# Small constant stores into the result, placed among the loads of a decode-attention kernel

## The chip, the core and the metric

The kernel runs on one core of a Trainium2 chip. A core has five engines that run their own instruction streams: PE (TensorE, matmul), DVE (VectorE), ACT (ScalarE), POOL (GpSimd) and SP (SyncE, which here only starts transfers). Transfers between HBM and the on-chip memory SBUF are done by 16 DMA engines. The metric is the device time of one execution in microseconds (us); lower is better.

## The reference

One decode step of a block in which attention and an MLP work on the same normalised input, and their results are summed:

```python
x = A_x                                   # 1 x 1 x 1024
xn = _layernorm(x, axis=-1)
return x + _A_ref(xn, A_k_cache, A_v_cache, A_wq, A_wo) + _B_ref(xn, B_w1, B_w2, B_w3, B_w4)

def _A_ref(x, k_cache, v_cache, wq, wo):  # 32 query heads, 4 key/value heads, 65536 cached positions, 128 wide
    q = x @ wq
    p = _softmax(q @ k * 128 ** -0.5)
    return (p @ v) @ wo
def _B_ref(x, w1, w2, w3, w4):
    x1 = x + shifted(_gelu(_layernorm(x) @ w1)) @ w2    # with one position only zeros are left of the shifted part
    return x1 + _gelu(_layernorm(x1) @ w3) @ w4
```

Everything is bfloat16 in HBM. The caches are 2 x 67 MB, the weights 36 MB; the result is 1024 values, 2 KB.

## The kernel before, in words

The kernel is written engine by engine. A helper `_op` puts an instruction on an engine's list and works out from buffer objects (`_B`) which semaphores it has to wait for; `_dma` does the same for a transfer, on SP's or ACT's list. A transfer's semaphore is named by a channel (`chan("k0")`), and each transfer adds 16 to it when it has landed. Lists are emitted in order, so an engine that waits holds up all that stands behind it on its list.

**Loads.** One SBUF tensor, `KV`, holds four slots: two of 4 MiB for K and two of 8 MiB for V. All loads but that of x are issued by SP, in this order: wq, the first K, the first V, the second K (before the loop), and then, in a loop over 32 tiles n, what `issue_k` (L341) and `issue_v` (L349) give out:

```python
if n % 2:
    issue_k((n + 3) // 2)
if n % 4 == 1:
    issue_v((n + 3) // 4)
```

A K load covers two tiles and a V load four. Each waits until its slot has been read: `issue_k` waits for `QK` (L511) of the tile that has just used the slot, and `issue_v` for `PV` (L557). The transfers that SP has started stand in one queue, q1, and ACT's in another, q10. Near the end of the loop the weights w1, w2 and w3 of the MLP take over freed slots (n == 29), then wo and the first part of w4 (n == 31); after the loop the three last parts of w4 (L327).

**A tile.** `Ttr` transposes the tile's part of K in place on DVE (four instructions, L501). `QK` multiplies it with the queries into `S_ps`. `stats1`, `MB` and `stats2` form the running maximum; `EXP` makes the exponentials on ACT (L539) and the correction factor. `PTr` permutes and transposes them; `PV` multiplies with V into `OT_ps`; `FLASH` copies on ACT (L565) and accumulates on POOL. The engines other than SP run the tiles as hardware loops: `q_act.mark()` and its like mark where a loop's bodies begin and end, and what an engine is given behind the last mark runs once, after its loop.

**The end.** The w1 product (L639) with its GELU (L480 to L486; the Tanh on ACT is L484), the w2 product (L647), the second layer norm, the heads' combination, w3 (L472) with another GELU, wo (L681), w4 (L460). DVE copies the sums into `orow` (L717), and SP stores `orow` as four rows of 256 values (L718):

```python
ev_out = _dma(q_sp, chan("out"), lambda e: e.dma_start(out=out[0, 0, :].rearrange("(j n) -> j n", j=4), in_=orow[0:97:32, :]), reads=[b_p[0]])
q_sp.wait(ev_out)
```

`ones_f` is a 128 x 128 float32 tile of ones that GpSimd fills at the start; `b_const` is the buffer object of all such constants.

Of the kernel before, what the change touches and what calls it, by code (L numbers as in the profile page):

```python
# [6 lines left out]
BF = mybir.dt.bfloat16  # L7
# [113 lines left out]
def _deps(q, reads, writes):  # L121
    need = {}
    for b in reads:
        for s, v in b.w.items():
            need[s] = max(v, need.get(s, 0))
    for b in writes:

        for s, v in (list(b.r.items()) if b.r and b.whole else list(b.w.items()) + list(b.r.items())):
            if not (q.in_order and s is q.sem):
                need[s] = max(v, need.get(s, 0))  # L130
    for s, v in need.items():
        q.wait((s, v))


def _done(ev, reads, writes, partial=False):
    for b in reads:
        b.add_read(ev)
    for b in writes:
        if partial:
            b.add_write(ev)  # L140
        else:
            b.set_write(ev)


def _op(q, fn, reads=(), writes=(), partial=False, tick=True):
    _deps(q, reads, writes)
    ev = q.op(fn, tick)
    _done(ev, reads, writes, partial)
    return ev
# [17 lines left out]
def _dma(q, chan, fn, reads=(), writes=(), partial=False):  # L167
    _deps(q, reads, writes)
    chan.n += 1
    ev = q.dma(fn, chan.sem, 16 * chan.n)  # L170
    _done(ev, reads, writes, partial)
    return ev


def bass_parallel_sum__gqa_block_cached__mixer_s_mlp__decode_kernel(
# [32 lines left out]
    with ExitStack() as es:  # L208
        E = es.enter_context

        def sb(name, shape, dt):
            return E(nc.sbuf_tensor(name, shape, dt))
# [4 lines left out]
        def sem(name):  # L217
            return E(nc.semaphore(name))

        ident_bf = sb("ident_bf", [P, P], BF)  # L220
        ones_f = sb("ones_f", [P, P], F32)
# [68 lines left out]
        q_act = _Q("act", sem("c_act"))  # L290
        q_pool = _Q("pool", sem("c_pool"))
        q_sp = _Q("sp", None)
# [5 lines left out]
        def chan(name):  # L298
            if name not in chans:
                chans[name] = _DmaChan(sem("d_" + name))  # L300
            return chans[name]

        b_const = _B("const")
# [39 lines left out]
        def issue_v(j):  # L343
            if j >= NV:
                return
            h, nb = divmod(j, NV // HKV)
            src = A_v_cache[0, h, nb * 4 * SUB:(nb + 1) * 4 * SUB, :].rearrange("(p c) d -> p (c d)", p=P)
            sl = j % 2
            _dma(q_sp, chan("v%d" % sl), lambda e: e.dma_start(out=KV[:, VOFF[sl]:VOFF[sl] + 32768], in_=src), writes=[b_V[sl]])  # L349
# [59 lines left out]
        for c0, n_, lhs, rhs in ((0, P, selGT[:, :], selGT[:, :]), (P, P, selGT[:, :], selPT[:, :]),  # L409
                                 (256, 4, selTT[:, :], ident_bf[0:4, 0:4]), (260, 16, selDT[:, :], ident_bf[0:16, 0:16])):  # L410
            _op(q_pe, lambda e, c0=c0, n_=n_, lhs=lhs, rhs=rhs: e.matmul(CM_ps[:, c0:c0 + n_], lhs, rhs, start=True, stop=True),
                reads=[b_const, b_pT], writes=[b_CM], partial=(c0 > 0))
# [23 lines left out]
        for h in range(HKV):  # L436
            for we in range(4):
# [3 lines left out]
                    reads=[b_M1, b_const], writes=[b_Y], partial=(h + we > 0))  # L441
# [50 lines left out]
        def Ttr(n, idx):  # L492
            if n >= NT:
                for ix in idx:
                    q_dve.op(lambda e, ix=ix: e.memset(spare[:, ix:ix + 1], 0.0))
                return
            s, half = (n // 2) % 2, n % 2
            for ix in idx:
                c = KOFF[s] // 2 + 4096 * half + 1024 * ix
                _deps(q_dve, [b_K[s][half]], [])  # L500
                ev = q_dve.op(lambda e, c=c: e.transpose(out=KV32[:, c:c + 1024], in_=KV32[:, c:c + 1024]))  # L501
                b_T[s][half].add_write(ev)

        def QK(n):
            s, half = (n // 2) % 2, n % 2
            fns = []
            for we in range(4):
                w_hi, e_ = divmod(we, 2)
                for cm in range(4):
                    mv = bass.AP(KV[:].tensor, KOFF[s] + half * 8192 + cm * 128 + w_hi * 64 + e_, [[kstep, P], [512, 16], [2, 32]])  # L510
                    fns.append(lambda e, we=we, cm=cm, mv=mv: e.matmul(  # L511
                        S_ps[32 * cm:32 * cm + 32, :], Ycur[:, we, :, :].rearrange("p a g -> p (a g)"), mv,
                        start=(we == 0), stop=(we == 3), tile_position=(0, 32 * cm)))
            _grp(q_pe, fns, reads=[b_T[s][half], b_Yc], writes=[b_S])

        def stats1(n):
            m = n % 2
            _op(q_dve, lambda e: e.reduce_max(mrow[:, m:m + 1], S_ps[:, :], axis=AX.X), reads=[b_S], writes=[b_mrow[m]])  # L518
            _op(q_dve, lambda e: e.tensor_tensor(out=Rm[:, m, :], in0=sel16[:, :], in1=mrow[:, m:m + 1].broadcast_to([P, 16]), op=ALU.mult),  # L519
                reads=[b_mrow[m], b_const], writes=[b_R[m]])  # L520

        def MB(n):
            m = n % 2
            _op(q_pe, lambda e: e.matmul(MB_ps[:, 0:16], Lmat[:, :], Rm[:, m, :], start=True, stop=True),  # L524
                reads=[b_R[m], b_const], writes=[b_MB])

        def stats2(n):
            _op(q_dve, lambda e: e.tensor_reduce(out=Bst[:, n % 4:n % 4 + 1], in_=MB_ps[:, 0:16], axis=AX.X, op=ALU.min),  # L528
                reads=[b_MB], writes=[b_Bcol[n % 4]])

        def EXP(n):
            m = n % 2
            ko = 1 - m
            cL = 513 * m
            if n % 4 == 0:
                q_dve.wait((s_b, n // 4 + 1))
            _op(q_dve, lambda e: e.tensor_tensor(out=brun[:, m:m + 1], in0=brun[:, ko:ko + 1], in1=Bst[:, n % 4:n % 4 + 1], op=ALU.min),  # L537
                reads=[b_brun[ko], b_Bcol[n % 4]], writes=[b_brun[m]])
            _op(q_act, lambda e: e.activation(p_sb[:, m, :], S_ps[:, :], ACTF.Exp, bias=brun[:, m:m + 1], scale=SCALE, accum_out=tmpO[:, cL:cL + 1]),  # L539
                reads=[b_S, b_brun[m]], writes=[b_p[m], b_tmpL[m]])  # L540
            _op(q_dve, lambda e: e.tensor_tensor(out=dd[:, m:m + 1], in0=brun[:, m:m + 1], in1=brun[:, ko:ko + 1], op=ALU.subtract),  # L541
                reads=[b_brun[ko], b_brun[m]], writes=[b_dd[m]])
            _op(q_act, lambda e: e.activation(ff[:, m:m + 1], dd[:, m:m + 1], ACTF.Exp), reads=[b_dd[m]], writes=[b_ff[m]])  # L543
# [48 lines left out]
        for n in range(NT):  # L592
            if n % NSUB == 0:
                q_pe.mark(const_sems)
                q_pool.mark()
            if n % 4 == 0:
                q_act.mark()
            if n % 4 == 2:
                q_dve.mark(const_sems)
            if n == 0 or n % 4 == 2:  # L600
                Ttr(n, range(4))
            ahead = n + 1 if n % 4 != 1 else None
            if n % 4 != 1:
                QK(n)
            if ahead:
                Ttr(ahead, [0])
            stats1(n)
            MB(n)
            stats2(n)
            EXP(n)  # L610
            if ahead:
                Ttr(ahead, [1])
            PTr(n)
            if ahead:
                Ttr(ahead, [2, 3])
            if n % NSUB == NSUB - 1:
                head_switch(n // NSUB + 1)
            if n % 4 == 0:
                QK(n + 1)
            PV(n)  # L620
            FLASH(n)
            if n % NSUB == NSUB - 1:
                head_end(n // NSUB)
            if n % 2:
                issue_k((n + 3) // 2)
            if n % 4 == 1:
                issue_v((n + 3) // 4)
            if n == NT - 3:
                load_at(KOFF[0], b_K[0][:1] + b_T[0], "w1", B_w1, 0, 8)
                load_at(KOFF[0] + 8192, b_K[0][1:], "w2", B_w2, 0, 8)  # L630
                b_epi.r.update(b_V[0].r)
                load_at(VOFF[0], [b_V[0]], "w3", B_w3, 0, 8)
            if n == NT - 1:
                load_at(VOFF[1], [b_V[1]], "wo", A_wo, 0, 32)
                load_at(KOFF[1], b_K[1] + b_T[1], "w40", B_w4, 0, 16)
        for q in (q_pe, q_pool, q_act):
            q.mark(const_sems)

        _grp(q_pe, [lambda e, j=j, q=q: e.matmul(M0_ps[32 * q:32 * q + 32, :], xn2_bf[:, j:j + 1].broadcast_to([P, 32]),  # L639
                                                 KV[:, j * D + 512 * q:j * D + 512 * (q + 1)],  # L640
# [38 lines left out]
        def half_rows(items, reads):  # L679
# [12 lines left out]
            reads=[b_cb], writes=[b_keep])  # L692
# [3 lines left out]
            reads=[b_OT, b_const], writes=[b_pT])  # L696
# [6 lines left out]
            reads=[b_M0, b_M1], writes=b_ge)  # L703
# [11 lines left out]
        out_rows(*w4_rows(2))  # L715
        out_rows(*w4_rows(3), last=True)
        _op(q_dve, lambda e: e.tensor_copy(orow, OUT_ps[:, 0:256]), reads=[b_OUT], writes=[b_p[0]])  # L717
        ev_out = _dma(q_sp, chan("out"), lambda e: e.dma_start(out=out[0, 0, :].rearrange("(j n) -> j n", j=4), in_=orow[0:97:32, :]), reads=[b_p[0]])  # L718
        q_sp.wait(ev_out)

# [33 lines left out]
```

## Time and profile before

| what | value |
|---|---|
| time, median of 2 runs | 400.58 us (400.48 to 400.67) |
| time of the profiled execution | 400.37 us |
| its span | 399.0 us |
| busy: PE, DVE, ACT, POOL | 44%, 59%, 12%, 23% of the span |
| read from HBM | 169.87 MB, 426 GB/s over the span |
| share of q1 (SP's transfers) in the DMA engines' time | 98.7% |
| from issue to landing, median: K, V | 23.7 us, 36.1 us |

The profile shows one execution. Its span runs from the first to the last recorded instruction; the time of the same execution is 1.4 us longer. Engines are named as above, and PEld is PE's weight load; "SPq" is SP issuing a transfer, which ends long before the transfer lands. A row of digits gives the busy share in 40 equal slices of the span, in tenths. The chain of waits follows the work that ended last back to its beginning; a "DMA" piece in it runs from the issue of a transfer to its landing, so it holds the time in the queue too. A packet is one contiguous piece that one DMA engine moves; besides the data there are 4-byte packets that increment the transfer's semaphore.

### The profile page before, as it was taken

How to read it: one execution, taken by the hardware profiler on the slowest of the kernel's cores; microseconds unless marked ns; L12 is line 12 of the kernel's file. 1: busy time of each engine (PE TensorE's matmuls, PEld its weight loads, DVE VectorE, ACT ScalarE, POOL GpSimd, SP SyncE). 2: the span in 40 equal slices, each digit the busy share in tenths (PEclk: the TensorE clock that was granted, in tenths of full speed). 3: DMA queues.
4: the chain of work that ended last, by engine and by line, in shares of the span. 5: the costliest groups of instructions: out<-in, count | busy, mean ns of one | idle time of the engine just before them, and what ended most of it. 6: DMA issues, size and time to landing. Idle time of an engine off the chain costs nothing.

```text
span 399.0 us, 4487 instructions
## 1 busy us (share of the span) xinstructions
PE 175.9 (44%) x1456; PEld 53.1 (13%) x1456; DVE 235.4 (59%) x403; ACT 49.1 (12%) x132; POOL 91.6 (23%) x173
## 2 busy tenths in 40 slices
PE   0044244455254525442544464245426442572775
PEld 0022111111011101110111111011101110121322
DVE  0024756784688388728864886487657756635411
ACT  1000020111021101110201020111021120110000
POOL 6000012232135212230253021304331222251000
PEclk9997555555556656665655556656555655567699
DMA  8989999999999999999999999999999999999995
GB/s 355 486 368 473 416 418 424 434 429 443 470 422 394 447 440 420 427 447 466 427 407 434 440 420 440 434 466 427 411 430 440 434 434 406 456 459 421 419 409 247
DMA packets 4912, 169.98 MB, mean 426 GB/s; under 512 B 676, under 2 KB 680, under 8 KB 808
## 3 DMA queue, kind: packets, MB, share of 16 engines
q1 hardware_dynamic: 4760, 169.87, 98.7%
q8 instruction: 5, 0.08, 0.1%
q10 hardware_dynamic: 144, 0.00, 0.0%
q14 instruction: 3, 0.02, 0.0%
HBM read 169.87 MB, written 0.00 MB: 426 GB/s over the span
## 4 chain that ended last, share of the span: by engine, by line
DMA 57%; DVE 18%; PE 13%; issue 10%; ACT 1%; another core or an unknown queue 0%; POOL 0%; DVEq 0%; SPq 0%; ACTq 0%; POOLq 0%
DMA KV<-in_A_k_cache_dram 42%; DVE KV L501 13%; DMA KV<-in_B_w_dram 9%; PE S_ps L511 8%; DMA x_bf<-in_A_x_dram 6%; DVE mrow L518 2%; PE PT_ps L547 2%; PE OT_ps L557 1%; PE MM_ps L639 1%; ACT p_sb L539 1%; DVE pT_f L549 1%; PE MB_ps L524 1%; PE MM_ps L647 0%; DVE Rm L519 0%
## 5 line engine op out<-in xcount | busy, mean ns | idle before, releaser
L501 DVE STREAM_TRANSPOSE KV<-KV 128x1024 f32<-128x1024 f32 x128 | 149.5, 1211 | 23.9 <-DMA KV<-in_A_k_cache_dram 23.9
L511 PE MATMUL S_ps<-KV,Ycur 128*32 128x512 bf16 x512 | 59.5, 613 | 84.4 <-DVE KV L501 84.0
L570 POOL TENSOR_TENSOR O_acc<-O_acc,tmpO 128x513 f32<-128x513 f32 x32 | 40.8, 1275 | 121.9 <-ACT tmpO L565 121.9
L557 PE MATMUL OT_ps<-KV,pT_f 128*32 128x512 bf16 x512 | 58.9, 610 | 19.5 <-DVE pT_f L549 18.7
L518 DVE TENSOR_REDUCE mrow<-S_ps 128x1 f32<-128x512 f32 x32 | 22.1, 691 | 38.4 <-PE S_ps L511 38.4
L539 ACT ACTIVATE p_sb<-S_ps,brun 128x512 bf16<-128x512 f32 x32 | 22.0, 687 | 137.7 <-DVE brun L537 137.7
L547 PE MATMUL PT_ps<-p_sb,permR 128*128 128x512 bf16 x32 | 17.3, 541 | 44.5 <-ACT p_sb L539 44.5
L565 ACT ACTIVATE tmpO<-OT_ps 128x512 f32<-128x512 f32 x32 | 19.2, 599 | 136.8 <-PE OT_ps L557 78.3
L511 PEld LDWEIGHTS S_ps<-KV,Ycur 128*32 128x32 bf16 x512 | 14.4, 126 | 125.3 <-DVE KV L501 96.3
L549 DVE STREAM_TRANSPOSE pT_f<-PT_ps 128x512 f32<-128x512 f32 x32 | 22.7, 709 | 12.1 <-PE PT_ps L547 11.4
L567 POOL TENSOR_TENSOR spare<-ff 128x1 f32<-128x1 f32 x32 | 6.2, 193 | 102.0 <-ACT ff L543 100.3
L568 POOL TENSOR_SCALAR O_acc<-O_acc,ff 128x514 f32<-128x514 f32 x32 | 22.4, 701 | 0.0
L557 PEld LDWEIGHTS OT_ps<-KV,pT_f 128*32 128x32 bf16 x512 | 15.7, 130 | 50.6 <-DVE pT_f L549 28.9
L524 PE MATMUL MB_ps<-Rm,Lmat 128*128 128x16 bf16 x32 | 6.1, 191 | 25.3 <-DVE Rm L519 25.3
L528 DVE TENSOR_REDUCE Bst<-MB_ps 128x1 f32<-128x16 f32 x32 | 5.6, 174 | 14.2 <-PE MB_ps L524 14.2
L389 PE MATMUL MM_ps<-ln_s,ones_f 128*128 128x1 f32 x6 | 1.8, 362 | 27.0 <-DVE ln_s L388 27.0
L385 DVE CAST xT<-x_bf 128x8 f32<-128x8 bf16 x1 | 0.2, 170 | 21.3 <-DMA x_bf<-in_A_x_dram 21.3
L401 POOL TENSOR_TENSOR ln_s<-ln_s,neghalf 128x1 f32<-128x1 f32 x3 | 1.7, 558 | 40.5 <-DVE ln_s L399 40.5
L524 PEld LDWEIGHTS MB_ps<-Rm,Lmat 128*128 128x128 bf16 x32 | 3.3, 102 | 52.5 <-DVE Rm L519 52.5
L547 PEld LDWEIGHTS PT_ps<-p_sb,permR 128*128 128x128 bf16 x32 | 3.2, 101 | 47.3 <-ACT p_sb L539 47.3
L541 DVE TENSOR_TENSOR dd<-brun 128x1 f32<-128x1 f32 x32 | 5.7, 178 | 3.6
L537 DVE TENSOR_TENSOR brun<-brun,Bst 128x1 f32<-128x1 f32 x32 | 5.5, 172 | 3.7
(117 smaller groups left out, 123.4 us busy)
## 6 DMA issues: line engine op xcount, KB each, us to landing
KV<-in_A_k_cache_dram SPq DMA_DIRECT2D x16, 4096.0 KB, 23.7
KV<-in_B_w_dram SPq DMA_DIRECT2D x1, 7168.0 KB, 33.7
KV<-in_B_w_dram SPq DMA_DIRECT2D x2, 2048.0 KB, 15.1
KV<-in_B_w_dram SPq DMA_DIRECT2D x1, 4096.0 KB, 34.8
KV<-in_B_w_dram SPq DMA_DIRECT2D x1, 1536.0 KB, 34.0
KV<-in_B_w_dram SPq DMA_DIRECT2D x1, 1024.0 KB, 36.0
KV<-in_B_w_dram SPq DMA_DIRECT2D x1, 512.0 KB, 36.8
KV<-in_A_v_cache_dram SPq DMA_DIRECT2D x8, 36.1
```

The costliest lines, as they stand in the source:

```text
L501: ev = q_dve.op(lambda e, c=c: e.transpose(out=KV32[:, c:c + 1024], in_=KV32[:, c:c + 1024]))
L511: fns.append(lambda e, we=we, cm=cm, mv=mv: e.matmul(S_ps[32 * cm:32 * cm + 32, :], Ycur[:, we, :, :].rearrange("p a g -> p (a g)"), mv, s ...
L518: _op(q_dve, lambda e: e.reduce_max(mrow[:, m:m + 1], S_ps[:, :], axis=AX.X), reads=[b_S], writes=[b_mrow[m]])
L524: _op(q_pe, lambda e: e.matmul(MB_ps[:, 0:16], Lmat[:, :], Rm[:, m, :], start=True, stop=True), reads=[b_R[m], b_const], writes=[b_MB])
L539: _op(q_act, lambda e: e.activation(p_sb[:, m, :], S_ps[:, :], ACTF.Exp, bias=brun[:, m:m + 1], scale=SCALE, accum_out=tmpO[:, cL:cL + 1]) ...
L547: _op(q_pe, lambda e: e.matmul(PT_ps[:, :], permR[:, :], p_sb[:, m, :], start=True, stop=True), reads=[b_p[m], b_const], writes=[b_PT])
L549: _op(q_dve, lambda e: e.transpose(out=pT_f[:, :], in_=PT_ps[:, :]), reads=[b_PT], writes=[b_pT])
L557: fns.append(lambda e, q=q, q4=q4: e.matmul(OT_ps[32 * q4:32 * q4 + 32, :], pT_bf[:, q, :, 1], KV[:, v0 + 512 * q:v0 + 512 * (q + 1)], sta ...
L565: _op(q_act, lambda e: e.activation(tmpO[:, 1:513], OT_ps[:, :], ACTF.Copy), reads=[b_OT], writes=[b_tmpO])
L567: q_pool.op(lambda e: e.tensor_tensor(out=spare[:, 4:5], in0=ff[:, m:m + 1], in1=ff[:, m:m + 1], op=ALU.add), False)
L568: b_Oacc.set_write(q_pool.op(lambda e: e.tensor_scalar(out=O_acc[:, :], in0=O_acc[:, :], scalar1=ff[:, m:m + 1], scalar2=0.0, op0=ALU.mult ...
L570: ev = q_pool.op(lambda e: e.tensor_tensor(out=O_acc[:, m:m + 513], in0=O_acc[:, m:m + 513], in1=tmpO[:, m:m + 513], op=ALU.add), tick=(s_ ...
```

## The change

In tile 17, behind the loads of that tile, SP issues six stores of parts of `ones_f` into the result; ACT issues a seventh behind its loop. The shapes differ: four rows from partitions 0, 32, 64, 96; four rows from neighbouring partitions; one row; 16 rows; 128 rows of 4 bytes; and again four rows from partitions 0, 32, 64, 96. In all they write 2,048 bytes. Before the final store, which writes the whole result, SP waits for both channels, so the constants are overwritten.

```diff
             if n % 4 == 1:
                 issue_v((n + 3) // 4)
+            if n == 17:
+                o1 = out[0, 0, :]
+                for a, src in ((0, ones_f[0:97:32, 0:16]), (128, ones_f[0:4, 0:16]), (256, ones_f[0:1, 0:64]), (384, ones_f[0:16, 0:4]), (512, ones_f[:, 0:1]),
+                               (768, ones_f[0:97:32, 16:32])):
+                    rows = src.bitcast(BF)
+                    dst = o1[a:a + rows.shape[0] * rows.shape[1]].rearrange("(j n) -> j n", j=rows.shape[0])
+                    ev_o1 = _dma(q_sp, chan("o1"), lambda e, rows=rows, dst=dst: e.dma_start(out=dst, in_=rows), reads=[b_const], writes=[_B()])
...
         for q in (q_pe, q_pool, q_act):
             q.mark(const_sems)
+        ev_o2 = _dma(q_act, chan("o2"), lambda e: e.dma_start(out=out[0, 0, 896:1024].rearrange("(j n) -> j n", j=4), in_=ones_f[0:97:32, 0:16].bitcast(BF)),
+                     reads=[b_const], writes=[_B()])
...
         _op(q_dve, lambda e: e.tensor_copy(orow, OUT_ps[:, 0:256]), reads=[b_OUT], writes=[b_p[0]])
+        q_sp.wait(ev_o1)
+        q_sp.wait(ev_o2)
         ev_out = _dma(q_sp, chan("out"), ...)
```

## The prediction

> **What bounds the kernel now.** I read the page first (its rows of slices and its table of queues), then the chain of waits, then SP's timeline around the place of the change, then the end. The page:
>
> ```profile
> span 399.0 us, 4487 instructions
> DMA  8989999999999999999999999999999999999995
> DMA packets 4912, 169.98 MB, mean 426 GB/s; under 512 B 676, under 2 KB 680, under 8 KB 808
> q1 hardware_dynamic: 4760, 169.87, 98.7%
> q10 hardware_dynamic: 144, 0.00, 0.0%
> ```
>
> The 16 DMA engines are busy in nine tenths or more of nearly every slice, and 98.7% of their time goes to one queue, q1, which SP fills. The chain of waits shows what hangs on it (columns: start, length, what):
>
> ```profile
> 230.32 1.93 PE S_ps L511 x16
> 232.33 23.78 DMA KV<-in_A_k_cache_dram
> 256.13 0.06 DVE KV L501
> ...
> 269.04 1.93 PE S_ps L511 x16
> 271.05 23.75 DMA KV<-in_A_k_cache_dram
> ...
> 359.63 36.78 DMA KV<-in_B_w_dram
> ```
>
> The chain names PE and DVE between the loads, but those steps only set when a load is put into the queue. When it lands is set by what stands ahead of it. A load of K is 4 MiB and a load of V 8 MiB; one round of four tiles is two of K and one of V, 16.78 MB, and K landings in the chain lie 38.7 us apart (256.11 and 294.80): 433.8 GB/s. By that rate 4 MiB takes 9.7 us, so of the 23.8 us of the load issued at 232.33 some 14 us are waiting in the queue. The weights go on in the same way: between 333.4 (last K) and 396.4 (last part of w4) 27.26 MB move, 432.8 GB/s. The queue is thus never empty from the second load to 396.4, and a microsecond that the slowest DMA engine loses anywhere in it comes out at the end. That engine is the resource; compute has slack.
>
> **The change, part by part.** It removes nothing. It adds six stores on SP behind the loads of n == 17, one store on ACT behind its loop, and two waits on SP ahead of the final store.
>
> *The issue on SP.* SP's timeline around the place, and the end:
>
> ```profile
> 209.83 0.33 SPq L341 DMA_DIRECT2D KV<-in_A_k_cache_dram  x1
> 210.21 0.42 SPq L349 DMA_DIRECT2D KV<-in_A_v_cache_dram  x1
> ...
> 232.33 0.33 SPq L341 DMA_DIRECT2D KV<-in_A_k_cache_dram  x1
> ...
> 397.36 0.62 SPq L718 DMA_DIRECT2D out_dram<-p_sb  x1
> ```
>
> The loads at 209.83 and 210.21 are issue_k(10) and issue_v(5) of n == 17 (the eleventh K, the sixth V); the next, issue_k(11), leaves at 232.33 when QK(19) has freed its slot. SP is idle from 210.63 to 232.33, 21.7 us. A store's issue is the last row: 0.62 us; six are 3.7 us, done by 214.4. What is queued behind them on SP is issue_k(11) alone, which is not due for another 17.9 us; were that cover gone, its 14 us in the queue would still hide 3.7 us. Cost 0. The constants were written by GpSimd in the first 10 us, so the wait for them passes at once.
>
> *The packets in q1.* A load of 128 rows is 128 packets and 16 increments of its semaphore: the x load alone makes q10's 144. The 33 loads of q1 (16 K, 8 V, wq, wo, 7 parts of B's weights) make 33 x 144 = 4752; the final store's four rows make the other 8, four rows and four increments. So the stores of 4, 4, 1, 16, 128 and 4 rows add 8 + 8 + 2 + 32 + 144 + 8 = 202. The 128-row and 16-row stores reach all 16 engines: 8 + 1 and 1 + 1 = 11 packets on each. An engine that gets a row of every store carries 19. They stand between the sixth V, which lands at 210.21 + 36.1 = 246.3, and the K that lands at 256.11. The trace's packet records price small packets in this same busy queue: a 4-byte increment takes 9 ns and the next load's first packet begins 6 ns after it; x's 16-byte rows take 9 ns, among packets of 65,536 bytes; the final store's 512-byte rows take 28 to 32 ns. So 11 packets at 9 ns are 0.1 us on every engine, the slowest too, and 19 are 0.17 us. I take 0.1.
>
> *The write receipts.* This is what no row shows: a store into HBM with loads right behind it on the same engine. Its increment can only follow the landed row; whether the engine holds the next load meanwhile is open. The low bound is nothing: 33 loads have such an increment, in 6 ns each, and no later packet is lengthened (1213 ns for nearly all of 32 KB). The high bound is the final store, whose landing SP awaited:
>
> ```profile
> SPq L718 <- DVE p_sb L717: 37.3, 1, 37.3
> SPq L57 <- DMA out_dram<-p_sb: 1.0, 1, 1.0
> ```
>
> 1.0 us from the end of the issue; the packet records put 0.6 of it ahead of the first packet and 0.4 from the first packet to SP. Six in a row, each held for 1.0 us, are 6.0 us; held for 0.4, 2.4 us. There is a cover for some of it: the 16 engines do not finish together. The sixth V's increments run from 244.25 to 246.08 in the packet records, so an engine can be up to 1.8 us ahead, and a loss on it alone is free up to that lead. Between 0 and 6.0 I take 0.4, one receipt for the batch, since the loads' increments are the nearest row (same queue, same engines, same traffic) and they hold nothing.
>
> *A bound below nothing.* The lead of 1.8 us has a cause that the change might shift: the packet records show instruction fetches (q8, q14; 8 and 16 KB, 0.3 to 1.0 us each) at 44, 55, 85, 116, 366, 378 and 394 us, each on one engine beside its loads. A program a few instructions longer may fetch on other engines. If none fell on the slowest, the end would come up to 1.8 us sooner; one more would cost up to 1.0 us. I take 0.
>
> *The store on ACT, and the waits.* ACT around its place:
>
> ```profile
> 353.99 0.60 ACT L565 ACTIVATE tmpO<-OT_ps 128x512 f32<-128x512 f32 x1 [3.41 <-PE OT_ps L557]
> 359.80 0.63 ACT L484 ACTIVATE KV<-KV 64x512 f32<-64x512 f32 x1 [5.21 <-DVE KV L483]
> ```
>
> ACT issues at about 354.6 and then idles 5.2 us for DVE; the x load's issue on ACT took 0.40 us. Behind it stands the Tanh at 359.80, not late. On its engines q10 takes turns with q1: x's 9 packets per engine landed in 22.0 us, 2.4 us a turn, so one row and one increment are in by some 361 us. SP's two waits come after its issue at 359.2 and before the wait for L717 (37.3 us): both events are old by 397.36. Cost 0; if the ACT store were not in, the final store would wait for it, but it has 36 us.
>
> Sum: 0 + 0.1 + 0.4 + 0 + 0 = 0.5 us. The profiled execution took 400.37 us, of which 399.0 are span and 1.4 lie around it; it stands 0.2 below the median of 400.58. So the changed kernel's profile should show 400.9, and its median 401.1.
>
> **The rivals.** What this kernel's measurement can tell from no change is about 2%, 8.0 us.
>
> *Receipts one after another.* Every store's increment stops its engine until the row has landed, and one engine carries all six. For it: the ring is read in order. Against it: the 6 ns behind loads. With 1.0 us each it is 6.0 us, 406.6; with the 1.6 us from issue to landing, 9.7 us, 410.3. From 1.34 us a store it is over 2%.
> The Trainium skill ("DMA: Bandwidth & Descriptors", the section on the anatomy of one DMA) puts most of a transfer's fixed 2 us into the receipt of the write, heaviest for HBM. No row here shows 2 us; by that figure six would be, as an estimate, 12 us.
>
> *Short rows, on the other side: slower.* The place is the 128-row store: 8 rows of 4 bytes on every engine, all into the same 512 bytes. If a row so short is read, merged and written back before the next, every engine, the slowest too, pays 8 round trips, and one more for the 16-row store. At the final store's 1.0 us that is 9.0 us, 409.6; with the other four stores on one engine 13.0, 413.6. It decides from 0.9 us a row. For it: no write this small is in the trace. Against it: packets of 4 and 16 bytes at 9 ns, though reads or increments.
> The Trainium skill (same page, Specifications) says that below 512 bytes the DMA engine does a read-modify-write. Only the final store, at just 512 bytes a row, is shown here.
>
> *Nothing, or a little gain.* All loss falls into the lead, or the fetches shift: 398.8 to 400.6.
>
> *Late loads.* The stores hold SP or the queue so long that issue_k(11) is late past its 14 us of backlog. The six would need 21.7 + 14 us instead of 3.7; then the cost would start from there. That the change does nothing is no separate case: its packets must appear.
>
> **How the numbers follow.** Forecast (0.2 to 3 us more): 0.58. Nothing or a little gain: 0.14. Receipts in a row: 0.14, of it 0.06 over 2%. Short rows: 0.10. Anything else: 0.04, half on each side of 2%. So slower by over 2% is 0.06 + 0.10 + 0.02 = 0.18; faster 0.02, since the queue already moves 433.8 GB/s and 8 us would need 2% more; within 2% 0.80. The range starts at 399.5, inside the gain case, and ends at 408.6, past receipts at 1.0 us; it leaves out some 0.16 above and 0.04 below. The forecast's own range is 400.6 to 403.6.
>
> **What would show it right or wrong.** Right: SP shows six issues between 210.6 and 215 and still idles until its next K at about 232.3; that K lands at 256.1 to 257; q1 counts 4962 packets and q10 152; K landings further on are again 38.7 us apart; the last weight lands near 397. Receipts or short rows: the K behind the stores lands at 262 or later, all after it by as much, and the slice at 246 to 256 us moves fewer GB/s. Late loads: SP's issues run past 232. The forecast is wrong if the K issued at 232.3 takes over 27 us to land, or if the time is lost or won after 350 us, at ACT's store or the final one.

## The result, and the profile after

| | before | after |
|---|---|---|
| time, median | 400.58 us | 405.70 us (405.28 to 406.12) |
| profiled execution: time, span | 400.37, 399.0 us | 406.12, 404.9 us |

The ratio is 1.0126, 95% interval 1.0109 to 1.0143: 5.1 us slower, clear of noise and inside 2%. The page of the changed kernel:

```profile
span 404.9 us, 4496 instructions
DMA  9989999999998999999999999999999999999995
GB/s 395 434 372 456 416 435 479 421 410 421 434 474 388 427 460 421 444 421 456 434 408 424 482 427 169 434 460 421 427 431 463 434 401 419 463 452 422 413 412 234
q1 hardware_dynamic: 4962, 169.88, 98.7%
q10 hardware_dynamic: 152, 0.00, 0.0%
```

The packets are the 202 and 8 that were counted ahead. The row of busy digits hides what happened: the DMA engines look as busy as before. The row of GB/s shows it: the slice from 243 to 253 us, the 25th, moves 169 GB/s, where its neighbours move over 400. In the same row of the kernel before, the 25th slice moves 440:

```profile
GB/s 355 486 368 473 416 418 424 434 429 443 470 422 394 447 440 420 427 447 466 427 407 434 440 420 440 434 466 427 411 430 440 434 434 406 456 459 421 419 409 247
```

The chain of waits of the changed kernel names the load that lost the time. Its loads from 193 us on (start, length, what):

```profile
193.68 23.72 DMA KV<-in_A_k_cache_dram
232.35 29.00 DMA KV<-in_A_k_cache_dram
276.29 23.73 DMA KV<-in_A_k_cache_dram
314.96 23.74 DMA KV<-in_A_k_cache_dram
363.51 38.55 DMA KV<-in_B_w_dram
```

The K load issued at 232.35, the one behind the six stores, takes 29.00 us instead of 23.78. The loads after it take 23.7 us again, but start later by what was lost. That one load explains 5.2 us.

SP's timeline shows that its own time is not the cause (start, length):

```profile
211.31 2.79 SPq L634 DMA_DIRECT2D out_dram<-ones_f  x6
...
232.35 0.37 SPq L341 DMA_DIRECT2D KV<-in_A_k_cache_dram  x1
```

Six issues in 2.8 us, then 18 us of idling until the next K, which leaves at the same moment as before. The busy time of the engines between 246 and 256 us, of before and after, has the DMA rate in its last column:

```profile
246.00:256.00 10.00, 5.17 (x50) 1.63 (x50) 2.47 (x7) 2.00 (x5) 3.39 (x4) 0.67 0.99 426
```
```profile
246.00:256.00 10.00, 5.17 (x50) 1.59 (x50) 2.33 (x7) 1.99 (x5) 3.39 (x4) 0.67 0.92 203
```

The trace's packet records go one step further. The stores' packets are short: 9 ns for 4 and 16 bytes, 11 for 64, 18 for 256, all between 244.2 and 246.2 us. The packets of loads next to and behind them are long: 36 packets of 32 KB take more than the usual 1.213 us, up to 6.7 us, and all engines are at their old pace again between 253.1 and 254.1. At 250.6 us 16 such packets are under way, as many as there are engines, each 3.5 to 6.7 us long. So the length recorded for a store's packet does not hold the time until its row has landed; that time shows in the loads. That the record is of the reading side, and that the loads wait behind rows still to be written, is an inference.

### The profile page after: what moved, and what is told of

Same layout as the page of the kernel before. It is cut to its first block, busy times and chain, and to the rows that moved or that the text cites. A ratio compares the mean times of both kernels' runs of the same rounds, so it can differ in the third digit from the quotient of the medians.

```text
span 404.9 us, 4496 instructions
## 1 busy us (share of the span) xinstructions
PE 171.8 (42%) x1456; PEld 52.2 (13%) x1456; DVE 235.4 (58%) x403; ACT 49.0 (12%) x132; POOL 92.1 (23%) x173
## 4 chain that ended last, share of the span: by engine, by line
DMA 57%; DVE 18%; PE 13%; issue 9%; ACT 1%; another core or an unknown queue 1%; POOL 0%; DVEq 0%; SPq 0%; ACTq 0%; POOLq 0%
DMA KV<-in_A_k_cache_dram 42%; DVE KV L501 13%; DMA KV<-in_B_w_dram 10%; PE S_ps L511 8%; DMA x_bf<-in_A_x_dram 5%; DVE mrow L518 2%; PE PT_ps L547 2%; PE OT_ps L557 1%; ACT p_sb L539 1%; DVE pT_f L549 1%; PE MB_ps L524 1%; PE MM_ps L648 1%; PE MM_ps L656 0%; DVE Rm L519 0%
## 5 line engine op out<-in xcount | busy, mean ns | idle before, releaser
L557 PE MATMUL OT_ps<-KV,pT_f 128*32 128x512 bf16 x512 | 56.5, 589 | 19.5 <-DVE pT_f L549 18.7
L690 PE MATMUL S_ps<-KV,o_bf 128*1 128x512 bf16 x64 | 7.1, 379 | 3.4 <-DMA KV<-in_A_wo_dram 3.4
## 6 DMA issues: line engine op xcount, KB each, us to landing
KV<-in_A_k_cache_dram SPq DMA_DIRECT2D x16, 4096.0 KB, 23.7
```

The costliest lines, as they stand in the source:

```text
L557: fns.append(lambda e, q=q, q4=q4: e.matmul(OT_ps[32 * q4:32 * q4 + 32, :], pT_bf[:, q, :, 1], KV[:, v0 + 512 * q:v0 + 512 * (q + 1)], sta ...
L690: _grp(q_pe, [lambda e, lhs=lhs, rhs=rhs, jj=jj: e.matmul(S_ps[32 * jj:32 * jj + 1, :], lhs, rhs[:, 512 * jj:512 * jj + 512], start=False, ...
```

## The experiments

In all of them the measure is the K load behind the stores, "the load", in the chain of waits: 23.78 us before, 29.00 in the changed kernel. This length also holds the moment of issue, which shifts a little from run to run. As a check, the increments in the traces give the time from the landing of the K that filled the same slot before it, 38.7 us in the kernel before; by it the losses below come out the same within 0.03 us, but for two that are named.

The edits shown are against the kernel before, those of the second block against the first block; `dst` is in the result unless the line says otherwise. In each kernel SP waits for the added store before it issues the final one. The first two kernels ran 4 and 10 times, all others once; the kernel before took 400.48 to 400.63 us beside them.

**Which store?** Only the 128 rows of 4 bytes, as in the edit, and the changed kernel without these, its other stores as they were:

```diff
+            if n == 17:
+                src = ones_f[:, 0:1].bitcast(BF)
+                dst = out[0, 0, 512:768].rearrange("(j n) -> j n", j=128)
+                ev_o1 = _dma(q_sp, chan("o1"), lambda e, src=src, dst=dst: e.dma_start(out=dst, in_=src), reads=[b_const], writes=[_B()])
```

> Of the seven stores only the one of 128 rows of 4 bytes is left (and SP's wait for it). In the changed kernel the K load issued at 232.35 us landed after 29.00 us, 5.3 us later than the 23.7 us of the other rounds. Theory A (short rows: the 128 rows of 4 bytes are the cost, whatever stands beside them): that load takes 28 to 29 us and the time is 404.5 to 405.7 us. Theory B (receipts in a row: every store of the six holds its engine until its rows have landed): one store of six is left, so at most a sixth of the loss, the load takes 23.7 to 24.6 us and the time is 400.5 to 401.5 us.

> All of the change but the store of 128 rows: five stores on SP (4, 4, 1, 16 and 4 rows) and the one on ACT. Theory A (short rows in great number): next to nothing is left; 29 rows of 16 to 256 bytes instead of 157, so by rows at most 29/157 of 5.3 us = 1.0 us; the K load behind the stores takes 23.7 to 24.8 us, time 400.5 to 401.6 us. Theory B (receipts in a row): five of six are left, 4.4 us; the load takes about 28 us, time about 405 us.

The chain of the first and of the second:

```profile
232.17 28.52 DMA KV<-in_A_k_cache_dram
```
```profile
232.79 23.74 DMA KV<-in_A_k_cache_dram
```

The 128-row store alone: 405.32 us, ratio 1.0123 (1.0106 to 1.0140). All the rest together, the ACT store included: 400.65 us, ratio 1.0001 (0.9992 to 1.0011). The loss is the 128-row store's, and receipts in a row are ruled out: five stores one behind the other in a full queue cost nothing that can be measured. Nor is a loss hidden in the lead of one engine: in the packet records the five stores' packets begin within 20 ns of each other on the engine that has rows of all, and behind them one load packet of 32 KB takes 1.275 us, all others 1.213. Beside the 128 rows they add something, 29.00 against 28.52 us.

**Where do the rows go?** The same rows 16 bytes apart, the same rows into SBUF, and later 8 bytes apart:

```diff
-                dst = out[0, 0, 512:768].rearrange("(j n) -> j n", j=128)
+                dst = out[0, 0, :].rearrange("(j n) -> j n", j=128)[:, 0:2]         # 16 bytes apart
+                dst = align_t[:, 0:2]                                                # an SBUF tile
+                dst = out[0, 0, 0:512].rearrange("(j n) -> j n", j=128)[:, 0:2]      # 8 bytes apart
```

> Only the store of 128 rows of 4 bytes, but the rows are 16 bytes apart and so spread over the whole 2,048 bytes of the result instead of 512. Theory A1 (each short row costs by itself, about 5.3 us / 128 = 41 ns, wherever it goes): the K load behind it takes 28 to 29 us, as with the rows side by side. Theory A2 (the rows wait for each other because they go into the same few bytes): four times the bytes, so the loss shrinks, to between a quarter (1.3 us) and a half (2.7 us) of it; the load takes 25 to 26.4 us.

> The same 128 rows of 4 bytes at the same place in the queue, but into SBUF (an unused tile) instead of HBM. Theory A (writes of short rows into HBM are what is slow): nothing is left but 9 packets an engine; the K load behind takes 23.7 to 23.9 us, time 400.4 to 400.9 us. Rival (any transfer of 128 four-byte rows costs this much, by its packets, its issue, or the turn from stores to loads): the load takes 28 to 29 us, time about 405 us.

> Only the store of 128 rows of 4 bytes, rows 8 bytes apart: spread over 1,024 bytes. Known so far: over 512 bytes (rows side by side) the load behind it took 28.5 us instead of 23.8 (4.7 us lost), over 2,048 bytes 23.9 (0.1 lost). Theory A2a (rows that go into the same short stretch wait for each other, one after another, and the loads stand only once more of them wait than can be put by): halving the density takes away more than half; by a straight line through the two known points (16 and 4 rows per 64 bytes) 8 rows per 64 bytes lose 1.6 us, the load takes 25.4 us. Rival A2b (only rows that touch each other, side by side with no gap, are slow, by a merge or a clash of neighbours): rows with gaps lose nothing, as at 16 bytes apart; the load takes 23.7 to 24.0 us.

The chains, in this order:

```profile
232.32 23.90 DMA KV<-in_A_k_cache_dram
```
```profile
232.39 23.79 DMA KV<-in_A_k_cache_dram
```
```profile
232.25 25.75 DMA KV<-in_A_k_cache_dram
```

Times 401.01, 400.63 and 402.27 us. The same 128 packets, the same bytes, the same source: over 512 bytes of HBM they cost 4.7 us, over 1,024 bytes 2.0 (1.8 from landing to landing), over 2,048 bytes 0.1, into SBUF, where each row goes to a partition of its own, nothing. So it is neither the number of packets nor their length, but how densely they fall in HBM. The expectation for 8 bytes was a line through two points (25.4); 25.75 is close to it, and that rows must touch to be slow is ruled out.

**Do they wait for each other, or for the loads?** The same store with nothing else under way, at the end, ahead of the final store:

```diff
+        ev_o1 = _dma(q_sp, chan("o1"), lambda e: e.dma_start(out=out[0, 0, 512:768].rearrange("(j n) -> j n", j=128), in_=ones_f[:, 0:1].bitcast(BF)),
+                     reads=[b_const, b_p[0]], writes=[_B()])
+        q_sp.wait(ev_o1)
         ev_out = _dma(q_sp, chan("out"), ...)
```

> The store of 128 rows of 4 bytes side by side stands at the very end: SP issues it when the result is ready, waits for it, and then stores the result. No load is under way. Its own landing is measured by SP's wait. The final store of four rows takes 1.0 us from the end of its issue. Theory A2c (the rows wait for each other, with or without loads): its wait is about 1 + 5 to 8 us, the time 407 to 410 us. Rival A2d (the rows are slow only against the reads of the loads): its wait is 1.0 to 1.6 us, the time 402 to 402.6 us (0.6 us of issue on top).

SP's waits in it (us in total, times, longest):

```profile
SPq L721 <- DMA out_dram<-ones_f: 6.6, 1, 6.6
...
SPq L57 <- DMA out_dram<-p_sb: 1.0, 1, 1.0
```

407.52 us. 512 bytes as 128 rows land 6.6 us after the end of the issue, while 2,048 bytes as four rows take 1.0. No load has a part in it: the rows wait for each other.

The same store behind ACT's loop, in q10, where its rows come one by one between packets of loads:

```diff
+        ev_o2 = _dma(q_act, chan("o2"), lambda e: e.dma_start(out=out[0, 0, 512:768].rearrange("(j n) -> j n", j=128), in_=ones_f[:, 0:1].bitcast(BF)),
+                     reads=[b_const], writes=[_B()])
```

> The store of 128 rows of 4 bytes side by side is issued by ACT behind its loop instead of by SP, so it stands in q10, and the engines take turns between it and the loads of q1: one row, then one packet of a load (57 to 64 KB, 2.1 to 2.4 us). The 8 rows of an engine are spread over some 18 us, 128 rows at one in 0.14 us, where in q1 they all came within 2 us. Theory A2 (rows wait for each other at their place in HBM, 5 us / 128 = 40 ns each, and the loads stand while they do): rows that come more slowly than they are taken do not pile up; nothing lost, 400.4 to 401.0 us. Rival (every short row stops its engine or all engines for its own time, however far apart they come): the same 4.7 us, 405 us.

The last weight in its chain:

```profile
359.90 38.03 DMA KV<-in_B_w_dram
```

It lands at 397.93, 1.5 us later than before (396.41); the time is 402.03. Neither expectation was met: a third of the loss stays. The packet records say where: the first two rows of an engine go together, and the 16 load packets that begin between 359.0 and 361.2 us are each 0.2 to 0.8 us too long, 8.9 us in all. But 41 packets behind them add another 11.5 us, although the rows by then come some 0.2 us apart; in the kernel before, two packets there add 1.0. Taking turns is not what costs: x's rows, which go into SBUF, alternate with load packets in the same way in the kernel before, and from 2.5 to 30 us no load packet is longer for it. Spacing helps; it does not cure, and rows that wait for each other by 44 ns do not explain what is left. That is open.

**How big is the place, and does it matter who writes?** Four kernels: eight pieces from each of 16 partitions, to eight different stretches of 64 bytes; the same pieces in touching clusters of four, one every 64 bytes; 16 rows alone; two stores into separate 512 bytes:

```diff
+                src = ones_f[0:16, 0:16:2].unsqueeze(2).bitcast(BF)                  # 8 pieces a partition, 64 bytes apart
+                dst = out[0, 0, 512:768].rearrange("(i j n) -> j i n", i=8, j=16)
...
+                dst = out[0, 0, :].rearrange("(j a k) -> j a k", j=16, a=2)[:, :, 0:8].rearrange("j a (b n) -> j a b n", n=2)   # clusters
...
+                src, dst = ones_f[0:16, 0:1].bitcast(BF), out[0, 0, 512:544].rearrange("(j n) -> j n", j=16)
...
+                for a in (0, 512):
+                    dst = out[0, 0, a:a + 256].rearrange("(j n) -> j n", j=128)
```

> 128 pieces of 4 bytes that fill the same 512 bytes, from 16 partitions with 8 pieces each, ordered so that the 8 pieces of one DMA engine go to 8 different stretches of 64 bytes, and each stretch gets one piece from each of 16 engines. [...] Theory A2 by the place (what counts is how many pieces go into a stretch, whoever sends them): the loss stays, 4 to 6 us, the load behind takes 28 to 30 us. Rival (an engine's own successive rows into one stretch wait for each other): the pieces of one engine are 64 bytes apart, as far as nothing was lost with 16 bytes; the loss goes, the load takes 23.7 to 24.2 us.

> 128 pieces of 4 bytes in 32 clusters of four that touch each other (16 bytes), one cluster every 64 bytes over the 2,048 bytes of the result: four pieces in each 64 bytes, as with rows 16 bytes apart, but as dense within 16 bytes as in the slow store. How big is a place? Theory 64 (a place is 64 bytes or more): 4 pieces a place, loss 0.1 to 0.3 us, the load takes 23.8 to 24.1 us. Rival 16 (a place is 16 bytes, or touching neighbours are what is slow): loss 4 to 5 us, the load takes 28 to 28.8 us. With places of 32 bytes it lies between: 4 of the 8 rows of the slow store, about 2 us, the load takes 25.8 us.

> Only 16 rows of 4 bytes, one from each DMA engine, side by side in one stretch of 64 bytes. A place gets 16 rows, as in the store of 128 rows, but there is only one place. Theory 64 (a place is 64 bytes and takes 0.4 us for each row): the last row is in after 16 x 0.4 = 6.4 us; if the rows waiting hold all engines, the load behind is late by 4 to 5 us, 28 to 29 us. Rival 512 (a place is 512 bytes or the whole store, 128 rows at 0.05 us): 16 rows are 0.8 us, nothing lost, the load takes 23.7 to 23.9 us. A third way: the places are 64 bytes, but the engines stand only once many rows wait (one row an engine doesn't fill what they can put by): nothing lost too, though the rows are late.

> Two stores of 128 rows of 4 bytes side by side, into two separate stretches of 512 bytes, one behind the other in q1. So far the load behind is late by 4.7 us at 16 rows per 64 bytes, 2.0 at 8 and 0.1 at 4: a line of about 0.4 us for each row that goes into the same 64 bytes, less some 1.5 us that is put by. Theory P (rows wait for rows of their own place, and different places are served side by side): each place still gets 16 rows, the loss stays near 4.7 us, up to 6; the load takes 28.5 to 29.8 us. Rival (all short rows pass one after another through one point, 5 to 6 us for 128): twice the rows, 4.7 + 6 us; the load takes 34 to 35 us.

The chains, in the order of the edits:

```profile
232.29 27.16 DMA KV<-in_A_k_cache_dram
```
```profile
232.22 24.24 DMA KV<-in_A_k_cache_dram
```
```profile
232.13 24.49 DMA KV<-in_A_k_cache_dram
```
```profile
232.23 30.01 DMA KV<-in_A_k_cache_dram
```

Times 404.08, 400.91, 401.15 and 407.36 us. Mixed over the engines, 3.4 us are lost, below the 4 to 6 expected, but most of the 4.7: what counts most is the place, and an engine's own order is at best the rest. Touching clusters over 2,048 bytes lose 0.5 us (0.1 to 0.3 expected): the place is not as small as 16 or 32 bytes. The two together also speak against rows that wait only for rows of their own engine. If an engine takes the pieces of one partition, places of up to 64 bytes would have cost the first kernel nothing, and larger ones the second, where these pieces lie within 80 bytes, the whole 4.7 us. Which engine took which rows the records do not say. Two stores into two places lose 6.2 us, a little over the 4.7 to 6 expected, and far from the 10.7 of a single point for all rows. From the first row at 244.4 us to the last increment at 251.7 it is some 7 us, where the 128 rows alone take 5.5 (below) and twice that would be 11. So two places are served side by side for the most part, not wholly.

The 16 rows into 64 bytes tell most through their own landing, in the view of the transfers (KB of one, us from issue to landing): 16 rows alone, 128 rows side by side, and 8 bytes apart:

```profile
out_dram<-ones_f SPq DMA_DIRECT2D x1, 0.1 KB, 35.5
```
```profile
out_dram<-ones_f SPq DMA_DIRECT2D x1, 0.5 KB, 39.0
```
```profile
out_dram<-ones_f SPq DMA_DIRECT2D x1, 0.5 KB, 36.4
```

With the issues at 211.27, 211.15 and 210.90 they land at 246.8, 250.1 and 247.3 us. Rows begin at 244.1 to 244.2 and the last engine's come at 246.0 to 246.3 in all three; an increment of a load is seen some 0.33 us after its packet. So 128 rows into 512 bytes keep their place busy for 5.5 us, 43 ns each; at the end of the kernel, from the first packet at 398.50 to the landing at 404.59, less the 0.33, for 5.8 us, 45 ns each. At 8 bytes apart, 64 rows to each 512 bytes need 2.8 us: 44 ns again. But 16 rows into 64 bytes are in when the last one comes: the last increment is seen 0.50 us after its packet, and 0.46 with the rows that go into SBUF. Were a place 64 bytes, its 16 rows would need the 5.5 us, and even at 128 bytes (32 rows in 5.5 us) half of that, 2.8 us, and land at 247.3. So the place is larger than 128 bytes. It is smaller than 1,024, since rows 8 bytes apart went faster. 256 or 512 bytes is open, and with 256 a row would take 88 ns. Why 16 rows that land at once still cost the load something is open too. By its length it is 0.7 us, from landing to landing 0.35, since it was issued earlier; the 18 load packets that are too long, by up to 0.7 us, all begin after 246.6 us, when 15 of the 16 rows are in.

**Rows of 16 bytes**, 128 of them side by side over the whole result:

```diff
+                src, dst = ones_f[:, 0:4].bitcast(BF), out[0, 0, :].rearrange("(j n) -> j n", j=128)
```

> A store of 128 rows of 16 bytes side by side, over the whole 2,048 bytes: four rows in each 64 bytes, as with 4-byte rows 16 bytes apart, but no byte between them left out. Theory P (what counts is how many rows go into one place): loss 0.1 to 0.3 us, the load takes 23.8 to 24.1 us, time 400.5 to 401.0 us. Rival (any store of 128 short rows that touch each other): loss 4 to 5 us, the load takes 28 us or more, time 405 us.

```profile
232.26 24.22 DMA KV<-in_A_k_cache_dram
```

401.12 us; 0.4 us lost by the load, a little above the expectation, a tenth of the 4-byte store's. Four times the bytes in the same number of rows cost a tenth, because they fall over four times the space.

## Why the prediction was right and where it was not

The measured 405.7 lies in the range and within 2%, but 401.1 was its likeliest value, with 400.6 to 403.6 as its own range: right sign, a tenth of the size. That the time lies in the range is luck: the range went up to 408.6 to take in receipts in a row, which the runs rule out. The prediction's own sign of a wrong forecast, over 27 us for the K issued at 232.3, came with 29.00.

- **What bounds the kernel: right.** What the engines lost from 246 us on came out at the end, 5.2 us at the load and 5.1 in the median time. The lead of 1.8 us between engines covered nothing, since 16 load packets stood at once.
- **Issue on SP: right.** 2.8 us instead of 3.7, wholly in SP's idle time.
- **Packets in q1: right, and beside the point.** 202 packets of 9 to 18 ns. I took these lengths for the price of a row, while the price is paid by later packets.
- **Write receipts: this term failed.** I took 0.4 us of the 0 to 6.0 for the whole batch. For the five other stores zero was right (ratio 1.0001), so the loads' increments were a good row for them. For the 128-row store no row of before stood: the only write into HBM there is the final store's four rows of 512 bytes. I priced the store by its packet count, where its destination decides: 128 rows through one place at some 44 ns.
- **Short rows: the right store, the wrong mechanism.** This rival named the place, and gave 9.0 us by eight round trips of 1.0 us on every engine. There are no such round trips on an engine: 16-byte rows and spread 4-byte rows cost 0.4 and 0.1 us. The rows wait for each other across the engines, and part of the wait is absorbed without loss: 5.5 us of it held the loads for 4.7, 2.8 us for 1.8 to 2.0, and some 1.4 us (an estimate: 32 rows at 44 ns) for 0.1 to 0.5. The Trainium skill's read-modify-write below 512 bytes ("DMA: Bandwidth & Descriptors", Specifications) would fit writes that can't overlap in one place, but no run shows it, and length alone did not cost: 29 rows of 16 to 256 bytes were free.
- **Receipts in a row: wrong.** It had the size nearest to the result (6.0 us at 1.0 each), by another cause. By the Trainium skill's 2 us for a transfer's fixed cost (same page, the anatomy of one DMA, which it gives for transfers that GpSimd issues), five stores that each hold their engine for it would have shown, as an estimate, 10 us; none of it held the queue.
- **ACT store and waits: right.** In the changed kernel ACT's issue overlaps its copy, and the Tanh still waits for DVE (start, length, and the idle time before it in brackets):

```profile
358.97 1.08 ACTq L645 DMA_DIRECT2D out_dram<-ones_f  x1
363.60 0.63 ACT L484 ACTIVATE KV<-KV 64x512 f32<-64x512 f32 x1 [4.25 <-DVE KV L483]
```

- **Instruction fetches: no shift showed.** In the packet records of the changed kernel the fetches are as many and as long, at the same stages. On which engine each falls the records do not say. From the landing of the last K to that of the last weight the changed kernel takes 63.4 us and the one before 63.0; what made the difference is open.

## What to carry to other kernels

A small store in a full load queue is free by the count of its packets and can still stop every DMA engine: look at where in HBM its rows land. A column stored from 128 partitions, 4 bytes from each, into one stretch of 512 bytes cost about 5 us in the loads' own queue, 1.5 us in another queue that takes turns with it, and 7 us when the end of the kernel waited for it; one row of 256 bytes or four rows of 64 cost nothing that could be measured. When DMA busy stays at nine tenths and the kernel is slower, read the row of GB/s and the landing time of the load behind the suspect, not the busy share.

## What the runs showed of the hardware that I had not expected

Short rows written into the same stretch of HBM, 256 or 512 bytes, waited for each other: 128 rows of 4 bytes took 5.5 to 5.8 us, some 44 ns each if the stretch is 512 bytes, with loads under way or without. Two stretches were served mostly side by side. Meanwhile the loads stood: packets of 1.213 us took up to 6.7 us. With the 128-row store alone, at 250.0 us, 14 of its 16 increments are in and 16 load packets, as many as there are engines, are still standing. The last increment is seen at 250.1, and these load packets end between 251.3 and 253.1. The first 1 to 1.5 us of such waiting cost the loads little, 0.1 to 0.5 us, when the rows came in one burst. What in the path to HBM makes the rows wait no run shows.
